# Pair 0 opens with its last 256 queries, and ScalarE's queue carries both one-hot rows

## The chip, the cores and the metric

The kernel runs on one core of one Trainium2 chip. The metric is device time in microseconds (us), the median of several executions of the whole kernel. Five engines work side by side, each on its own list of instructions in order: TensorE (PE in the profile, with PEld for its weight loads), VectorE (DVE), ScalarE (ACT), GpSimd (POOL) and SyncE (SP), which here only starts transfers. ACT and POOL start transfers too. An engine that has to wait for another's result holds up everything behind it in its own list. PSUM is the memory that TensorE writes its results to; it has eight banks of 512 fp32 values per partition.

## The reference, cut to what matters

Attention over 4 batches of 8 heads, 768 positions, head dimension 64, with a block mask, and then a mixer on its output:

```
scores = scale * q @ k.T                       # per batch and head, 768 x 768
mask   = |blk_i - blk_j| <= 1, or first/last block, or a sampled block   # blocks of 32
attn   = softmax(where(mask, scores, -1e9));   attn_out = attn @ v
u      = x + (U @ V applied over the sequence to x)      # x: heads side by side, rank 32
out    = u + relu(u @ w_ch1) @ w_ch2                     # 512 -> 2048 -> 512
```

Three random key blocks per query block (`sampled_blocks`) come in as data, so the mask is made on the chip.

## The kernel before, in words

**Pairs and units.** Two heads are handled together as a pair: 16 pairs, four of them (`HP`) to a batch. The diff touches pair 0, the first of all. The score matrix of a pair is computed transposed, keys on the partitions, in nine units (`NU`, `parts`, L474): with `tr, kind = divmod(u, 3)`, kinds 0 and 1 are one key tile of 128 against queries 0 to 511 (`QA`), and kind 2 is two key tiles against the last 256 queries (`QB`). A unit's scores for both heads fill one PSUM tile of 128 x 2 x 512 (`scores`, L480), two such tiles alternate during the first batch, and one exponential on ACT (L497) turns a unit into fp16 weights `est`. The values follow three units later (`VLAG`, `flush_value`, L898): 8 matmuls per unit against `vt`, accumulated in two PSUM buffers `pav`, one for queries 0 to 383 and one for 384 to 767. `norm` (L533) divides them by their row sums on DVE after the last two units.

**The mask.** In the first batch it is added inside the score matmul. The query operand `qa` has the head's 64 rows of q in one half of the partitions (`rows`) and in the other half (`mrows`) the mask rows, 24 per head: 0 where a query may look at a key block, -240 where it may not. The key operand `ka` has k in the one half and in the other the one-hot rows, which say which block a key belongs to. The one-hot rows are loaded from memory (`hot_rows`, L303); the mask rows come from a small matmul on PE (`mask_mm`, L374) of `cbd`, which DVE makes from `sampled_blocks`, into a PSUM tile `pm`, and are written to `qa` by DVE or ACT (`mask_rows`, L382). From the same two operands `mask_tiles` (L451) makes a mask `m01` of ones and zeros for the later batches: two matmuls `pmk` and two comparisons on DVE per key tile.

**How pair 0 starts.** q and k arrive as fp32 with positions on the partitions: `qld` in two loads, tiles 0 to 3 (`TQ`, 256 KB) and 4 to 5, `kld` in two loads, tiles 0 to 1 (`TK`) and 2 to 5. `cast0` (L326) makes fp16 copies `qst` and `kst` on DVE or POOL; PE turns them tile by tile into PSUM (`turn_some`, L263, into `pq` and `pk`); `half_copy` (L414) copies each head's half from there to `qa` or `ka`, on DVE or ACT. Unit 0 needs query tiles 0 to 3, key tile 0, the mask rows of queries 0 to 511 of both heads and both heads' one-hot rows. Matmuls named `warm` have no use but to keep PE busy.

**What sets the order.** Every engine's list is in program order (`keep`). In the first batch the loop at L1051 writes, for each pair and unit: the scores and the exponential, then the values of the unit three before, then the side work of `at_unit` (L983). In pair 0 that side work is: after unit 0 a warm matmul, the turns of the remaining q and k, the remaining mask rows, four half copies on DVE, then transfers on SP (`qa` mask rows to pair 1's `qa`, loads of pairs 2, U, V) and casts on POOL; after units 2, 3 and 8 a `mask_tiles`; after units 4 and 6 the turns of pair 1. The buffers of `pav`, and those of the turns, `pmk` and others (`ps`), rotate in the order of their requests (`pst_tile`, L109). From the second batch on a planner interleaves attention with the mixer's matmuls `pt` and `pch`; its lists are fixed when the program is built.

Of the kernel before, what the change touches and what calls it, by code (L numbers as in the profile page):

```python
# [17 lines left out]
P = 128  # L18
# [3 lines left out]
def kernel(  # L22
# [86 lines left out]
    def pst_tile(shape, dtype, name, tag):  # L109
        n = singles[tag][0]  # L110
        singles[tag].rotate(1)
        return psp[tag].tile(shape, dtype, tag=f"{tag}{n}", name=name)
# [150 lines left out]
    def turn_some(st, pt, t0, t1):  # L263
        for t in range(t0, t1):
            keep(
                nc.tensor.transpose(  # L266
                    out=pt[:, t, :],
                    in_=st[:, t].rearrange("p h d -> p (h d)"),
                    identity=id16,
                )  # L270
            )
# [31 lines left out]
    def hot_rows(eng, st, h, n):  # L303
        r0 = mrows[h].start
        keep(eng.dma_start(out=ka[st][h][r0 : r0 + n, :], in_=oh_dr.ap()[0:n]))
# [4 lines left out]
            in_=sampled_blocks.bitcast(I32),  # L310
        )
    )
    keep(nc.sync.dma_start(out=qld[:, :, 0:TQ], in_=q0[:, :, 0:TQ]))
    keep(nc.scalar.dma_start(out=small[0:32], in_=small_dr.ap()))
    keep(nc.scalar.dma_start(out=kld[:, :, 0:TK], in_=k0[:, :, 0:TK]))
    keep(nc.sync.dma_start(out=qld[:, :, TQ:T], in_=q0[:, :, TQ:T]))
    keep(nc.sync.dma_start(out=kld[:, :, TK:T], in_=k0[:, :, TK:T]))
    hot_rows(nc.scalar, 0, 0, NB)
    hot_rows(nc.sync, 0, 1, NB)
    keep(nc.scalar.activation(out=dummy, in_=zeros[:, 0:1], func=AF.Exp))  # L320
    for vt in vts:
        keep(nc.gpsimd.memset(vt[:, :, :, D : D + 1], 1.0))
# [3 lines left out]
    def cast0(eng, st, ld, t0, t1):  # L326
        keep(
            eng(
                out=st.rearrange("p t h d -> p h t d")[:, :, t0:t1],
                in_=ld[:, :, t0:t1],  # L330
            )
        )
# [41 lines left out]
    def mask_mm(o, a, e):  # L374
        mm(
            o,
            cbd.rearrange("z a c -> z (a c)"),
            small[:, a:e],
            True, True,
        )  # L380

    def mask_rows(eng, h, i, a, e):  # L382
        o = qa[0][h][mrows[h], a:e]
        if eng == "dve":
            keep(
                nc.vector.tensor_scalar(
                    out=o, in0=i[mrows[h]],
                    scalar1=-MASK_BIAS, scalar2=MASK_BIAS, op0=ALU.mult, op1=ALU.add,
                )
            )  # L390
        else:
            keep(
                nc.scalar.activation(
                    out=o, in_=i[mrows[h]],
                    func=AF.Copy, scale=-MASK_BIAS, bias=MASK_BIAS,
                )
            )

    pm0 = pscp.tile([P, 2, 512], FP32, tag="double0", name="pm")
    pm1 = pst_tile([P, QA], FP32, "pm", tag="pav")  # L400
    pm2 = pscp.tile([P, 2, 512], FP32, tag="double1", name="pm")
    mask_mm(pm0[:, 0, 0:QA], 0, QA)
    mask_mm(pm1, 0, QA)
    cast0(nc.vector.tensor_copy, qst, qld, 0, TQ)
    mask_rows("dve", 0, pm0[:, 0, 0:QA], 0, QA)
    mask_rows("act", 1, pm1, 0, QA)
    pq = pst_tile([P, T, P], FP16, "pturn", tag="ps")
    pk = pst_tile([P, T, P], FP16, "pturn", tag="ps")
    turn_some(qst, pq, 0, TQ)
    turn_some(kst, pk, 0, TK)  # L410
    mask_mm(pm2[:, 0, 0:QB], QA, S)
    warm_pe(2)

    def half_copy(eng, dst, h, pt, t0, t1):  # L414
        keep(
# [4 lines left out]
        )  # L420

    for h in range(2):
        half_copy(nc.vector.tensor_copy, qa[0], h, pq, 0, TQ)
        half_copy(nc.scalar.copy, ka[0], h, pk, 0, TK)
    cast0(nc.gpsimd.tensor_copy, qst, qld, TQ, T)
    cast0(nc.gpsimd.tensor_copy, kst, kld, TK, T)
    del lds[0, "q"], lds[0, "k"]
    for h in range(2):
# [38 lines left out]
    NU = 9  # L467
# [3 lines left out]
    def new_est():  # L471
        return epool.tile([P, 2, QA], FP16, tag="est", name="est")
# [93 lines left out]
    def new_pav(tag):  # L566
        return pst_tile([P, 3, 2, D + 1], FP32, "pav", tag)
# [330 lines left out]
    def flush_value():  # L898
        i, u, ests, pavs, xs, xh = pend.popleft()
        b, hp = divmod(i, HP)  # L900
        if u == 0:
            pavs.extend([new_pav("pav"), new_pav("pav")])
        for g, q0, q1, at in parts(u):
            for j in range(q0 // P, q1 // P):
                for h in range(2):
                    mm(
                        pavs[j // 3][:, j % 3, h, :],
                        weights(ests, g, j, h),
                        vts[b % 2][:, 2 * hp + h, g, 0 : D + 1],
                        u == 0 and j in (0, 3) and h == 0, g == T - 1, True,  # L910
                    )
        end = i == HP - 1
        if u == NU - 2:
            norm(i, 0, pavs[0], xs, xh, end)
        if u == NU - 1:
            norm(i, 1, pavs[1], xs, xh, end)
            box = {}
            uh = xpool.tile([P, T, P], FP16, tag="uh", name="uh")
            tails.extend(
                [  # L920
                    lambda: mix_a(i, xh, box, 0, "ps"),
                    lambda: mix_a(i, xh, box, 1, "ps"),
                    lambda: mix_h(i, 0, box["a"], xs, uh, "ps", end),
                    lambda: mix_h(i, 1, box["a"], xs, uh, "ps", end),
                ]
            )
            if end:
                tails.extend([lambda c=c: turn_u_half(i, uh, c) for c in range(2)])
            else:
                tails.append(lambda: turn_u_pe(i, uh, "ps"))  # L930
# [52 lines left out]
    def at_unit(i, u):  # L983
        if (i, u) in MASKS:
            mask_tiles(MASKS.index((i, u)))
        if i == 0:
            if u == 0:
                warm_pe(1)
                turn_some(qst, pq, TQ, T)
                turn_some(kst, pk, TK, T)  # L990
                for h in range(2):
                    mask_rows("dve", h, pm2[:, 0, 0:QB], QA, S)
                for nm, o, pt, t in (("q", qa[0], pq, TQ), ("k", ka[0], pk, TK)):
                    for h in range(2):
                        half_copy(nc.vector.tensor_copy, o, h, pt, t, T)
                for h in range(2):
                    keep(
                        nc.sync.dma_start(
                            out=qa[1][h][mrows[h], :], in_=qa[0][h][mrows[h], :]
                        )  # L1000
                    )
                issue(2, "q")
                keep(
                    nc.sync.dma_start(
                        out=uld, in_=moe_U.rearrange("(p t) r -> p (t r)", t=T)
                    )
                )
                issue(2, "k")
                for h in range(2):
                    keep(nc.sync.dma_start(out=mvld[h * R : h * R + R], in_=moe_V))  # L1010
                cast(1, "q")
                cast(1, "k")
                cast(1, "v")
            if u == 1:
                issue(2, "v")
            if u == 3:
                issue(3)
            if u == 6:
                cast(2, "q")
                cast_U()  # L1020
                cast(2, "k")
            if u == 4:
                turn_part(1, "q", 0)
                turn_part(1, "q", 1)
            if u == 6:
                turn_part(1, "k", 0)
                turn_part(1, "k", 1)
            return
        if u == 0 and i < 3:
            issue(i + 3)  # L1030
        if i == 1 and u == 2:
            cast_V()
            cast(2, "v")
        if i == 2 and u == 0:
            for h in range(2):
                keep(nc.sync.dma_start(out=Vd[rows[h]], in_=Vt[rows[0]]))
        if (i, u) in WLOADS:
            WLOADS[i, u]()
        if u in (1, 2, 3, 4):
            turn_part(i + 1, "qk"[(u - 1) // 2], (u - 1) % 2)  # L1040
        for _ in range({0: 1, 5: 2, 6: 1, 7: 1}.get(u, 0)):
            if tails:
                tails.popleft()()
        if u == 7:
            cast(i + 2, "q")
        if u == 8:
            cast(i + 2, "k")
        if u == 0 and i > 1:
            cast(i + 1, "v")

    for i in range(HP):  # L1051
        ests, pavs = [], []
        xs, xh = new_x()
        for u in range(NU):
            ests.append(new_est())
            scores(i, u, ests[u])
            pend.append((i, u, ests, pavs, xs, xh))
            if len(pend) > VLAG:
                flush_value()
            at_unit(i, u)  # L1060

# [197 lines left out]
```

## Time and profile before

| | us |
|---|---|
| median of 4 runs (lowest to highest) | 279.13 (278.54 to 279.55) |
| the profiled execution, and its span | 279.55, 277.8 |
| PE busy | 270.3 (97%) |
| DVE busy | 175.0 (63%) |
| ACT busy | 177.0 (64%) |
| POOL busy | 103.2 (37%) |
| first exponential of pair 0 starts | 8.31 |
| first `pt` matmuls (mixer, batch 0) | 45.62 |

The span is what the profile shows from its first to its last instruction; the profiled execution's time is 1.75 us more than it. In the lines that follow, a timeline row reads: start, duration, engine, line, operation, output<-inputs, shapes, and in brackets how long the engine was idle before and what ended that. `x2` means that two instructions are merged into the row. A row of the chain of waits reads: start, duration, what was waited for. A row of the stretches reads: from:to and length, then busy us (and instructions) of PE, PEld, DVE, ACT and POOL, the granted clock of PE, the busy share of the DMA engines and GB/s. "SPq" and "ACTq" mark a transfer's issue on that engine.

### The profile page before, as it was taken

The page shows a single profiled execution, that of the slowest core. Times are in us where ns is not written, and L with a number is a line of the kernel's source. Part 1 is how long each engine was busy: PE and PEld are TensorE (multiplying, and loading weights), DVE is VectorE, ACT ScalarE, POOL GpSimd, SP SyncE. Part 2 cuts the span into 40 slices and gives each one's busy share as a digit, 9 for nine tenths or more (in the row PEclk, how much of TensorE's full clock was granted, in tenths as well). Part 3 has the DMA queues.
Part 4 walks back from the last instruction along what each step waited for, and adds up shares of the span by engine and source line. Part 5 has one row for each costly group of instructions (what it writes and reads, how often), then busy time and mean ns, then how long its engine had stood idle before and what let it go on. Part 6 is the DMA issues. An engine that isn't in the chain of part 4 may idle for free.

```text
span 277.8 us, 8036 instructions
## 1 busy us (share of the span) xinstructions
PE 270.3 (97%) x3492; PEld 161.5 (58%) x3492; DVE 175.0 (63%) x285; ACT 177.0 (64%) x198; POOL 103.2 (37%) x137
## 2 busy tenths in 40 slices
PE   7899999999999999999999999999999999999995
PEld 2577775566656564657565565656565655565443
DVE  6767767888887987777756768777777441000112
ACT  4799996787987857694855749584886201654000
POOL 4669539406374735363604536361102020000000
PEclk9999999999999999999999999999999999999999
DMA  6999966999979999996890999995100323000222
GB/s 185 297 284 287 282 145 92 186 179 75 142 49 96 181 130 139 160 103 74 64 108 0 184 92 167 132 97 75 31 2 2 104 79 93 13 1 0 78 76 77
DMA packets 85520, 31.69 MB, mean 114 GB/s; under 512 B 75164, under 2 KB 83084, under 8 KB 85484
## 3 DMA queue, kind: packets, MB, share of 16 engines
q0 software_dynamic: 49824, 10.29, 43.2%
q1 hardware_dynamic: 35304, 20.66, 34.6%
q8 instruction: 27, 0.44, 0.7%
q10 hardware_dynamic: 356, 0.22, 0.3%
q14 instruction: 9, 0.07, 0.1%
HBM read 27.88 MB, written 6.29 MB: 123 GB/s over the span
## 4 chain that ended last, share of the span: by engine, by line
PE 92%; ACT 2%; DMA 2%; DVE 2%; POOL 1%; issue 1%; DVEq 0%; POOLq 0%
PE pch L173 30%; PE pt L173 30%; PE psc L173 14%; PE pav L173 13%; ACT est L497 2%; PE pa L173 2%; DMA ka<-onehot_const 2%; PE ph L173 1%; PE pturn L266 1%; PE pmk L173 1%; POOL xh L597 0%; PE puT L710 0%; DVE xh L540 0%; DVE xs L588 0%; POOL qst L247 0%
## 5 line engine op out<-in xcount | busy, mean ns | idle before, releaser
L497 ACT ACTIVATE est<-psc 128x1024 f16<-128x1024 f32 x144 | 143.0, 1028 | 46.3 <-PE psc L173 44.7
L173 PE MATMUL pt<-uT,w1t 64*128 64x384 f16 (+1 forms) x896 | 94.4, 324 | 0.0
L173 PE MATMUL pch<-w2t,tT 64*128 64x512 f16 (+3 forms) x688 | 93.6, 372 | 0.1
L518 DVE TENSOR_TENSOR est<-est,m 128x1024 f16<-128x1024 f16 x108 | 78.3, 740 | 18.1 <-ACT est L497 16.8
L173 PEld LDWEIGHTS <-w1t 64*128 64x128 f16 (+1 forms) x896 | 46.0, 95 | 36.2 <-PE pt L173 8.3
L173 PEld LDWEIGHTS <-tT 64*128 64x128 f16 (+1 forms) x688 | 38.2, 95 | 36.9 <-PE pch L173 1.6
L735 ACT ACTIVATE tT<-pt 128x768 f16<-128x768 f32 (+1 forms) x48 | 36.6, 773 | 26.0 <-PE pt L173 26.0
L173 PEld LDWEIGHTS <-est 128*128 128x128 f16 x1152 | 41.4, 97 | 10.9 <-issue 5.0
L173 PE MATMUL pav<-vt,est 128*128 128x65 f16 x1152 | 44.5, 193 | 0.1
L790 DVE TENSOR_TENSOR of<-xf,pch 128x1024 f32<-128x1024 f32 (+3 forms) x16 | 15.2, 951 | 42.7 <-PE pch L173 42.7
L173 PE MATMUL psc<-qT,kT 64*128 64x512 f16 (+1 forms) x288 | 40.6, 323 | 0.3 <-ACT est L497 0.3
L597 POOL CAST xh<-xs 128x768 f16<-128x768 f32 x12 | 10.4, 869 | 80.2 <-DVE xs L588 74.6
L683 POOL CAST uh<-xf 128x768 f16<-128x768 f32 x12 | 13.9, 1161 | 26.1 <-DVE xf L674 14.5
L173 PE MATMUL psc<-qa,ka 128*128 128x512 f16 (+1 forms) x96 | 21.7, 326 | 1.7 <-DMA ka<-onehot_const 1.3
L737 DVE TENSOR_SCALAR tT<-pt 128x768 f16<-128x768 f32 (+1 forms) x20 | 18.3, 917 | 5.9 <-PE pt L173 5.8
L173 PEld LDWEIGHTS <-kT 64*128 64x128 f16 x288 | 14.6, 94 | 12.5 <-issue 0.7
L261 POOL DMA_DIRECT2D vt<-in_v_dram x20 | 16.3, 820 | 2.8 <-DMA w2t<-in_moe_w_ch_dram 2.7
L261 POOL DMA_DIRECT2D qst<-in_q_dram x20 | 16.3, 819 | 0.1
L261 POOL DMA_DIRECT2D kst<-in_k_dram x20 | 16.3, 820 | 0.0
L588 DVE TENSOR_TENSOR xs<-pav,rcp 128x768 f32<-128x768 f32 x12 | 11.5, 958 | 1.2
L674 DVE TENSOR_TENSOR xf<-xs,ph 128x768 f32<-128x768 f32 x12 | 11.4, 951 | 1.2 <-PE ph L173 1.2
L173 PEld LDWEIGHTS <-ka 128*128 128x128 f16 (+1 forms) x108 | 8.7, 97 | 5.3 <-issue 3.7
(69 smaller groups left out, 129.6 us busy)
## 6 DMA issues: line engine op xcount, KB each, us to landing
out_dram<-of SPq DMA_DIRECT2D x9, 512.0 KB, 3.3
vld<-in_v_dram SPq DMA_DIRECT2D x6, 384.0 KB, 7.5
w1t<-in_moe_w_ch_dram POOLq DMA_DIRECT2D x4, 512.0 KB, 8.6
w2t<-in_moe_w_ch_dram POOLq DMA_DIRECT2D x4, 512.0 KB, 10.1
qld<-in_q_dram SPq DMA_DIRECT2D x5, 384.0 KB, 7.0
kld<-in_k_dram SPq DMA_DIRECT2D x5, 384.0 KB, 7.9
qst<-in_q_dram POOLq DMA_DIRECT2D x20, 96.0 KB, 4.1
kst<-in_k_dram POOLq DMA_DIRECT2D x20, 96.0 KB, 4.4
```

Source lines behind the costliest of these rows:

```text
L173: ins = nc.tensor.matmul(out, lhsT, rhs, start=start, stop=stop, skip_group_check=loose)
L261: keep(nc.gpsimd.dma_start(out=o[:, h], in_=src_of(nm, i)[:, h]))
L266: nc.tensor.transpose(out=pt[:, t, :], in_=st[:, t].rearrange("p h d -> p (h d)"), identity=id16,)
L497: keep(nc.scalar.activation(out=est, in_=psc, func=AF.Exp, scale=0.125))
L518: keep(nc.vector.tensor_tensor(out=o, in0=o, in1=m, op=ALU.mult))
L588: nc.vector.tensor_tensor(out=xs.rearrange("p (c j) (h d) -> p c (j h) d", c=2, h=2), in0=pv[:, :, :, 0:D], in1=rcp[:, :, :, None].broadca ...
L597: keep(nc.gpsimd.tensor_copy(out=xh, in_=xs))
L674: nc.vector.tensor_tensor(out=u.rearrange("p (c j) n -> p c j n", c=2), in0=xs.rearrange("p (c j) n -> p c j n", c=2), in1=ph[:, :, 0:HS]. ...
L683: keep(nc.gpsimd.tensor_copy(out=uh, in_=u))
L735: keep(nc.scalar.activation(out=o, in_=i, func=AF.Relu))
L737: keep(nc.vector.tensor_scalar_max(out=o, in0=i, scalar1=0.0))
L790: nc.vector.tensor_add(out=of, in0=xfs[b][:, sc : sc + nsc, n0:n1], in1=pch)
```

## The change

Pair 0's units run in the order 2, 0, 1, 3, 4, ... 8; the side work stays with the position in that order. So the first scores are those of key tiles 0 and 1 against queries 512 to 767, and the parts of q change places: tiles 4 and 5 are loaded first, cast by DVE and turned before the first scores; tiles 0 to 3 are cast by POOL and turned after them. The turns and copies of k's last four tiles move from the first position to the second. The one-hot rows of both heads are loaded from ACT's queue. ACT writes the mask rows of queries 0 to 511 for both heads, from one PSUM tile, so one mask matmul of 512 columns goes; DVE writes those of queries 512 to 767 for both, now before the first scores. One warm matmul moves. `pavs` becomes a dictionary whose buffers are requested when first written.

```diff
-    keep(nc.sync.dma_start(out=qld[:, :, 0:TQ], in_=q0[:, :, 0:TQ]))
+    keep(nc.sync.dma_start(out=qld[:, :, TQ:T], in_=q0[:, :, TQ:T]))
     keep(nc.scalar.dma_start(out=small[0:32], in_=small_dr.ap()))
     keep(nc.scalar.dma_start(out=kld[:, :, 0:TK], in_=k0[:, :, 0:TK]))
-    keep(nc.sync.dma_start(out=qld[:, :, TQ:T], in_=q0[:, :, TQ:T]))
+    keep(nc.sync.dma_start(out=qld[:, :, 0:TQ], in_=q0[:, :, 0:TQ]))
     keep(nc.sync.dma_start(out=kld[:, :, TK:T], in_=k0[:, :, TK:T]))
-    hot_rows(nc.scalar, 0, 0, NB)
-    hot_rows(nc.sync, 0, 1, NB)
+    for h in range(2):
+        hot_rows(nc.scalar, 0, h, NB)
...
-    pm0 = pscp.tile([P, 2, 512], FP32, tag="double0", name="pm")
-    pm1 = pst_tile([P, QA], FP32, "pm", tag="pav")
-    pm2 = pscp.tile([P, 2, 512], FP32, tag="double1", name="pm")
+    pm2 = pst_tile([P, QB], FP32, "pm", tag="pav")
+    pm0 = pscp.tile([P, 2, 512], FP32, tag="double1", name="pm")
+    mask_mm(pm2, QA, S)
     mask_mm(pm0[:, 0, 0:QA], 0, QA)
-    mask_mm(pm1, 0, QA)
-    cast0(nc.vector.tensor_copy, qst, qld, 0, TQ)
-    mask_rows("dve", 0, pm0[:, 0, 0:QA], 0, QA)
-    mask_rows("act", 1, pm1, 0, QA)
+    mask_rows("dve", 0, pm2, QA, S)
+    for h in range(2):
+        mask_rows("act", h, pm0[:, 0, 0:QA], 0, QA)
+    cast0(nc.vector.tensor_copy, qst, qld, TQ, T)
+    mask_rows("dve", 1, pm2, QA, S)
...
-    turn_some(qst, pq, 0, TQ)
+    warm_pe(1)
+    turn_some(qst, pq, TQ, T)
     turn_some(kst, pk, 0, TK)
-    mask_mm(pm2[:, 0, 0:QB], QA, S)
-    warm_pe(2)
+    warm_pe(1)
...
-        half_copy(nc.vector.tensor_copy, qa[0], h, pq, 0, TQ)
+        half_copy(nc.vector.tensor_copy, qa[0], h, pq, TQ, T)
         half_copy(nc.scalar.copy, ka[0], h, pk, 0, TK)
-    cast0(nc.gpsimd.tensor_copy, qst, qld, TQ, T)
+    cast0(nc.gpsimd.tensor_copy, qst, qld, 0, TQ)
...
-        if u == 0:
-            pavs.extend([new_pav("pav"), new_pav("pav")])
...
+                    opens = j // 3 not in pavs
+                    if opens:
+                        pavs[j // 3] = new_pav("pav")
...
-                        u == 0 and j in (0, 3) and h == 0, g == T - 1, True,
+                        opens, g == T - 1, True,
...
             if u == 0:
                 warm_pe(1)
-                turn_some(qst, pq, TQ, T)
-                turn_some(kst, pk, TK, T)
+                turn_some(qst, pq, 0, TQ)
                 for h in range(2):
-                    mask_rows("dve", h, pm2[:, 0, 0:QB], QA, S)
-                for nm, o, pt, t in (("q", qa[0], pq, TQ), ("k", ka[0], pk, TK)):
-                    for h in range(2):
-                        half_copy(nc.vector.tensor_copy, o, h, pt, t, T)
+                    half_copy(nc.vector.tensor_copy, qa[0], h, pq, 0, TQ)
...
             if u == 1:
+                turn_some(kst, pk, TK, T)
+                for h in range(2):
+                    half_copy(nc.vector.tensor_copy, ka[0], h, pk, TK, T)
                 issue(2, "v")
...
-        ests, pavs = [], []
+        ests, pavs = {}, {}
         xs, xh = new_x()
-        for u in range(NU):
-            ests.append(new_est())
+        for n, u in enumerate((2, 0, 1, *range(3, NU)) if i == 0 else range(NU)):
+            ests[u] = new_est()
             scores(i, u, ests[u])
...
-            at_unit(i, u)
+            at_unit(i, n)
```

## The prediction

> **What bounds the kernel now.** I read part 1 of the page (PE 270.3 of 277.8 us), then the stretches, then the chain of waits from the start in order of time, then the timelines of ACT, PE and DVE up to 12 us, where the diff lies. One row of the stretches:
>
> ```profile
> 48.40:277.80 229.40, 225.66 (x2927) 131.97 (x2926) 140.97 (x207) 136.79 (x153) 70.96 (x83) 1.00 0.77 91
> ```
>
> After 48.4 us PE is busy 225.66 of 229.40 us at full clock, with the same instructions in both kernels. So whatever the change does to the moment when PE gets there moves the end by as much. Before it, 36 exponentials on ACT go in step with PE: two PSUM tiles alternate, so unit n+2's scores wait for exp n. The chain from the start:
>
> ```profile
> 2.77 4.99 DMA ka<-onehot_const
> 7.76 0.14 issue
> 7.90 0.39 PE psc L173
> 8.29 0.02 issue
> 8.31 1.03 ACT est L497
> 9.35 0.04 issue
> 9.39 0.60 PE psc L173 x4
> ```
>
> The first exp starts at 8.31 because head 1's one-hot rows, issued by SP at 2.77, land 4.99 us later. ACT up to there:
>
> ```profile
> 1.88 0.59 ACTq L305 DMA_DIRECT2D ka<-onehot_const  x1
> 2.50 1.28 ACT L320 ACT_TABLE_LOAD   x1 [2.50 <-DVE ka L287]
> 3.79 0.20 ACT L320 ACTIVATE dummy<-m 128x1 f16<-128x1 f16 x1
> 4.85 0.59 ACT L393 ACTIVATE qa<-pm 64x512 f16<-64x512 f32 x1 [0.86 <-PE pm L173]
> 5.71 0.76 ACT L416 COPY ka<-pturn 64x256 f16<-64x256 f16 x2 [0.27 <-PE pturn L266]
> 8.31 4.97 ACT L497 ACTIVATE est<-psc 128x1024 f16<-128x1024 f32 x5 [1.84 <-PE psc L173]
> ```
>
> ACT's operands were ready at 6.47 (5.71 + 0.76) and it idled 1.84 us. Next PE, then DVE, behind that first exp:
>
> ```profile
> 8.11 0.38 PE L173 MATMUL warm<-m 128*128 128x512 f16 x1
> 8.33 0.27 PE L266 MATMUL pturn<-id,qst 128*128 128x128 f16 x2
> 8.44 0.39 PE L266 MATMUL pturn<-id,kst 128*128 128x128 f16 x4
> ```
>
> ```profile
> 8.64 0.61 DVE L416 COPY qa<-pturn 64x256 f16<-64x256 f16 x2 [1.18 <-PE pturn L266]
> 9.28 0.86 DVE L416 COPY ka<-pturn 64x512 f16<-64x512 f16 x2
> 10.29 1.02 DVE L459 TENSOR_SCALAR m<-pmk 128x384 f16<-128x384 f32 x2 [0.15 <-PE pmk L173]
> ```
>
> The reader should see here that the exps after the first are fed by DVE. The two key copies (9.28, 0.86) end at 10.14; the second pmk matmul and the scores of key tile 2 (10.46) stand behind them on PE, and the fourth exp follows at 11.11 (10.46, 0.61 for its two score matmuls, 0.04 to ACT), 0.97 after the copies. I call that end of the copies D.
>
> **The change, part by part.** First the moment K at which ACT ends the second ka copy.
>
> Second one-hot on ACT's queue: one more issue of 0.59. In the build it waits on the semaphore of the first load (small, landed 0.73 + 1.9 = 2.63 by the DMA view), so it runs 2.66 to 3.25. Behind it on ACT stand the table load (1.28, to 4.56) and dummy (0.20, to 4.77). The old cover, 0.86 us of ACT idle before L393, is gone.
>
> Mask rows 0..511 of both heads on ACT: two of 0.59 with 0.03 between starts and ends, to 6.01. Then the two ka copies, 0.76: K = 6.77. The spacing of dependent-free ACT work has two rows: the copies do not overlap (two in 0.76, each 0.36), exps do (1.02 long, next 0.92 later). Three overlaps of 0.1 would give 6.47, which is also the floor set by the key turns (5.71 + 0.76). I take 6.77, from the copies: same engine, same half of the partitions, PSUM source. ScalarE: Activation LUTs, section What ACT_TABLE_LOAD costs, says that back-to-back ACTIVATEs overlap by about 93 ns; the exps agree and the copies do not. By that rule K would be 6.49, and the sum below about 0.23 instead of 0.51.
>
> The landing of that one-hot: the first one on ACT's queue, issued at 1.88, was there when its reader started its weights at 6.13, so at most 4.25 us; by it the second lands by 6.91, by SP's row (4.99) at 7.65. PE needs it at K + 0.03. A landing at 6.91 would add 0.11 (start 0.14 after it, as 7.90 after 7.76); I take 0, since 6.13 was set by ACT's copy and not by the landing; 7.65 is kept for a rival. DMA: Bandwidth & Descriptors, section Issuing engines are not separate DMA queues, says that transfers of all issuing engines share the same 16 DMA engines and another issuer saves only issue time. That speaks against this move: by it the row keeps SP's 4.99, and the sum would be that of the rival, 1.36.
>
> SP loses one issue (0.43) and swaps its two q loads: the last 128 KB go first, the 256 KB land by 1.73 + 3.7 = 5.43. Its qa-to-qa copies wait for mask rows ready at 6.01 instead of 7.0. All SP work behind moves earlier; it feeds pair 1, whose first scores are at 16.3. I cost this at nothing.
>
> POOL casts the 512-element q part (0.61, the row of the same form) instead of 0.40: 5.43 to 6.05, needed by PE at K + 0.72 = 7.49. Its rest of k lands at 2.26 + 5.1 = 7.36, cast to 8.0, needed at 9.2. Two one-hot issues (1.21) and v (0.83) end at 10.1, first value matmul about 11.2. So over 1 us of cover each; a load over 1 us late would come through in full.
>
> DVE's early work: two masks 64x256 (0.42), a cast (at most 0.43), two copies (0.29 each), 1.9 us from about 4.4, done by 6.3, beside ACT. PE's removed 512-column mask matmul and moved warm matmuls lie before K, in time that PE idles. They do keep it busy: PE's first six warm matmuls take 0.46 each (2.74 in all), those from 5.62 on start 0.22 apart. Before, PE had six warm and two mask matmuls by 4.82; now it has six, 256 and 512 columns and one more warm in about the same time, so I use the fast rows. If PE were still slow, the 2,816 columns from K to D would take twice their 1.2 us.
>
> Now from K to D, each from a row:
> K + 0.17 head 1's first score (6.09 to 6.26 before); three 256-column starts of 0.11 (four take 0.60, one 0.27): 0.50; warm 0.22 (8.11 to 8.33): 0.72; four q turns 0.39 and 0.04 to DVE: 1.15; two 64x512 q copies 0.87: 2.02; head 1's scores of unit 0 0.17: 2.19 (second exp 0.41 later, K + 2.60 = 9.37); matmul spacing 0.22: 2.41; four k turns 0.39 and 0.04: 2.84; two k copies 0.86: 3.70. D = 6.77 + 3.70 = 10.47, against 10.14: **0.33 later**. The first exp starts early, at 7.46 (K + 0.50, 0.16 left of the last matmul's 0.27, 0.03 to ACT), but what is late next is unit 0: its turns now stand behind the first scores, its copies behind them, and the k turns behind its scores. Ends: K at 6.47 gives 0.03, a one-hot at 6.91 gives 0.44.
>
> Masks, values and later units keep their order, and PE runs without a gap from the fourth unit's scores at 10.46 to 12.23, so the 0.33 is carried.
>
> The value accumulators: pair 0 now opens the half of queries 384.. first, so it gets the first buffer, normalised last. Before, pair 1's first values:
>
> ```profile
> 19.52 0.18 PE pav L173 x6
> 19.70 0.04 issue
> 19.74 0.24 PE pav L173 x2
> ```
>
> Six matmuls ran while DVE finished, two waited. Now the six use the late buffer and all eight wait: **0.18 more**. Ends: 0 if DVE is done early; 0.76 if the reciprocal (0.20) and multiply (0.56) both stand open. I take 0.18, since DVE's order is unchanged. PE has no gap after it to give it back: the chain of waits runs on PE, piece on piece, from 15.3 to 39.9.
>
> Sum: 0.33 + 0.18 = **0.51 us**. The profiled execution would go from 279.55 (span 277.8 and 1.75 around it) to 280.06; it stood 0.42 above the median of 279.13, so the median goes to 279.64. About 0.3% (0.84 us) is what a measurement of this kernel can tell from no change; 0.51 is 0.18%.
>
> **Rivals.** *The one-hot lands late* (slower). At 7.65, head 1's first score starts 0.14 after it, 7.79 instead of 6.94: 0.85 more, in all 1.36, 280.5. For it: SP's row, 4.99. Against: SP's rows stood behind 640 KB of q and k, ACT's behind 179 KB. It decides from a landing after 6.8.
>
> *Pair 1 waits for the whole normalisation* (slower). 0.76 in place of 0.18: 1.09 in all, 280.2. For it: PE and ACT have no slack there. Against: the values come after unit 3's scores, which already hide most of it.
>
> *PE still slow at K* (slower): 1.2 more, in all 1.7, 280.8; for and against as above.
>
> *The first exp's lead is kept* (faster). At K = 6.47 it starts at 7.16, 1.15 before 8.31; less 0.18, 0.97 gained, 278.2. For it: ACT idled 1.84 us for this one row. Against: the second exp must follow within 0.92 for that, and the count above puts it 1.9 later.
>
> **How the numbers follow.** Forecast 0.52, late one-hot 0.20, whole normalisation 0.10, slow PE 0.05, lead kept 0.13. The forecast's own range is 279.1 to 280.1 (K from 6.47 to 6.9, spread of the medians); some 0.08 of its chance lies over 279.97. So within 0.3%: 0.44; slower 0.08 + 0.20 + 0.10 + 0.05 = 0.43; faster 0.13. The range of 8 in 10 goes from 278.5, which leaves out most of the faster case, to 280.8, past the late one-hot with 0.3 for spread and up to the slow PE.
>
> **What the profile after would show.** First exp near 7.5 and ACT idle about 0.9 before the second, near 9.4; k copies on DVE ending near 10.5; fourth exp near 11.45 (before 11.11); eight pav together after DVE in pair 1; the tail from the first pt matmuls 0.5 later. A first exp beyond 8 would show the late one-hot; k copies ending before 10.1 would show the lead kept. I would be wrong as well if a load behind POOL's casts came more than 1 us later.

## The result, and the profile after

| | before | changed |
|---|---|---|
| median (lowest to highest), us | 279.14 (278.36 to 280.62), 79 runs | 279.71 (279.28 to 282.53), 53 runs |
| profiled execution, and its span | 279.55, 277.8 | 279.76, 278.0 |
| PE busy, us | 270.3 | 270.2 |
| first exponential starts | 8.31 | 7.41 |
| 36th exponential, the last of pair 3, starts | 41.69 | 41.90 |

The ratio is 1.003, with a 95% interval of 1.0021 to 1.0039: slower by 0.57 us by the medians, where 0.51 was forecast (279.64). The means lie 0.83 us apart (280.04 and 279.21), which is the 0.3% of the ratio, because some executions of the changed kernel run late at a lower granted clock; they are treated with the warm matmuls below.

The row of the stretches of the changed kernel from 48.6 us on, PE's columns alone (busy us and instructions, granted clock, busy share of the DMA engines, GB/s):

```profile
48.60:278.00 229.40, 225.68 (x2927) 1.00 0.78 91
```

It answers to the row 48.40 to 277.80 of before: as many instructions and as much busy time in as long a stretch, 0.2 later. All of the difference is made before it. It also holds across the kernels below that ran at full clock: each profiled execution's time is its 36th exponential's start plus 237.86 to 237.93 us (41.69 and 279.55 before, 41.90 and 279.76 after, 40.69 and 278.55 for the fastest). So what follows is read from the starts of 36 exponentials.

ACT's timeline of the changed kernel:

```profile
1.86 1.00 ACTq L305 DMA_DIRECT2D ka<-onehot_const  x2
2.89 1.28 ACT L320 ACT_TABLE_LOAD   x1 [2.89 <-DMA w1t<-small_const]
...
4.63 1.21 ACT L393 ACTIVATE qa<-pm 64x512 f16<-64x512 f32 x2 [0.24 <-PE pm L173]
5.74 0.74 ACT L418 COPY ka<-pturn 64x256 f16<-64x256 f16 x2
7.41 1.02 ACT L499 ACTIVATE est<-psc 128x1024 f16<-128x1024 f32 x1 [0.92 <-PE psc L173]
9.19 1.94 ACT L499 ACTIVATE est<-psc 128x1024 f16<-128x1024 f32 x2 [0.76 <-PE psc L173]
11.30 2.07 ACT L499 ACTIVATE est<-psc 128x1024 f16<-128x1024 f32 x2 [0.18 <-PE psc L173]
```

The idle times in brackets are what to read: before, ACT idled 1.84 us ahead of the first exponential and then ran on without a gap (five in the row shown). Now it idles 0.92, 0.76 and 0.18. The first exponential came 0.90 earlier, and the fourth (11.30) 0.18 later. The chain of waits says why:

```profile
2.56 4.18 DMA ka<-onehot_const
6.75 0.14 issue
6.88 0.49 PE psc L173 x3
7.37 0.21 PE warm L173
7.58 0.24 PE pturn L266 x4
...
7.85 0.42 DVE qa L418
...
8.29 0.44 DVE qa L418
...
8.77 0.38 PE psc L173
9.15 0.24 PE pturn L266 x4
...
9.48 0.42 DVE ka L418
...
9.91 0.44 DVE ka L418
```

Head 1's one-hot row lands at 6.75 and gates the first scores. Behind them stand unit 0's four turns of q and their two copies, unit 0's scores, four turns of k and their two copies, in one line up to 10.35. The exponentials wait at each handover from DVE.

Later, in pair 1's fifth unit, the chain reads:

```profile
18.74 0.26 PE pav L173 x8
...
19.02 0.21 DVE rcp L537
...
19.25 0.57 DVE xs L542
...
19.86 0.42 PE pav L173 x8
```

All eight value matmuls stand behind the normalisation's multiply (`xs`), where before six ran while it finished and two waited.

### The profile page after: what moved, and what is told of

Same layout as the page of the kernel before. It is cut to its first block, busy times and chain, and to the rows that moved or that the text cites. A ratio compares the mean times of both kernels' runs of the same rounds, so it can differ in the third digit from the quotient of the medians.

```text
span 278.0 us, 8034 instructions
## 1 busy us (share of the span) xinstructions
PE 270.2 (97%) x3491; PEld 161.4 (58%) x3491; DVE 174.2 (63%) x284; ACT 177.7 (64%) x199; POOL 103.4 (37%) x137
## 4 chain that ended last, share of the span: by engine, by line
PE 85%; ACT 8%; DVE 2%; DMA 2%; issue 1%; POOL 0%; DVEq 0%; POOLq 0%
PE pch L173 30%; PE pt L173 30%; PE pav L173 11%; PE psc L173 10%; ACT est L499 8%; PE pa L173 2%; DMA ka<-onehot_const 2%; PE ph L173 1%; DMA w1t<-small_const 1%; POOL xh L599 0%; PE pmk L173 0%; DVE xh L542 0%; DVE xs L590 0%; DVE ka L418 0%; DVE qa L418 0%
## 5 line engine op out<-in xcount | busy, mean ns | idle before, releaser
L173 PE MATMUL psc<-qa,ka 128*128 128x256 f16 (+1 forms) x96 | 21.8, 326 | 1.7 <-ACT ka L418 0.5
```

The source lines that it names most:

```text
L173: ins = nc.tensor.matmul(out, lhsT, rhs, start=start, stop=stop, skip_group_check=loose)
```

## The experiments

The table has, for each profiled execution, the start of the first exponential, some distances between starts, and the distance from the first to the 36th. The smallest values in a column (0.98, 0.90, 0.90, 0.94) are taken as those with no added wait. "Time" is that execution's own.

| kernel | first | to 2nd | 3rd to 4th | 11th to 12th | 13th to 14th | 1st to 36th | 36th | time |
|---|---|---|---|---|---|---|---|---|
| before | 8.31 | 0.98 | 0.90 | 0.90 | 0.94 | 33.38 | 41.69 | 279.55 |
| before, second trace | 7.55 | 0.98 | 0.90 | 1.03 | 1.06 | 33.63 | 41.18 | 279.06 |
| both rows on ACT | 7.27 | 1.28 | 0.90 | 1.60 | 1.04 | 34.11 | 41.38 | 279.25 |
| changed | 7.41 | 1.78 | 1.20 | 0.90 | 1.12 | 34.49 | 41.90 | 279.76 |
| one row back on SP | 7.10 | 1.78 | 1.20 | 0.90 | 1.22 | 34.38 | 41.48 | 279.34 |
| buffers as before | 7.73 | 1.78 | 1.20 | 0.90 | 0.94 | 34.30 | 42.03 | 279.90 |
| k turned earlier | 7.47 | 1.78 | 0.90 | 0.90 | 1.12 | 34.07 | 41.54 | 279.43 |
| both undone, PE warmer | 7.53 | 1.78 | 0.90 | 0.90 | 0.94 | 33.88 | 41.41 | 279.29 |
| both rows on ACT, loads swapped | 7.15 | 1.64 | 0.90 | 0.90 | 0.94 | 33.54 | 40.69 | 278.55 |

**The kernel before once more** (no edit), to see whether its one profiled execution was typical.

> The kernel before, a second time, to see how far one trace of it stands for its runs. Theory A (the handover alone): the time is within 0.1% of before; its first exp starts within 0.3 us of 8.31 and the key copies on DVE end within 0.3 of 10.14, so the change's trace (10.35) is 0.2 later for good. Rival B (the profiled execution of before was a slow one): the one-hot rows on SP's queue land earlier here, the first exp starts before 8.0 and the key copies end before 9.9, so that the change costs 0.5 or more at that point. Rival C (PE's clock): the executions' granted clock stays above 0.995 in nearly all of them, where about a fifth of the changed kernel's lay between 0.988 and 0.994.

Measured: 279.33 (278.45 to 280.33, 12 runs), ratio 1.001 [0.9993, 1.0027]; the profiled execution took 279.06. DVE's copies in its timeline (in the first trace they began at 8.64 and 9.28):

```profile
7.88 0.61 DVE L416 COPY qa<-pturn 64x256 f16<-64x256 f16 x2 [0.61 <-PE pturn L266]
8.52 0.86 DVE L416 COPY ka<-pturn 64x512 f16<-64x512 f16 x2
```

Head 1's row, again from SP, landed 4.20 us after its issue (7.01) instead of 4.99 (7.76), and the whole front came 0.76 earlier: the key copies end at 9.38, not 10.14. At the 36th exponential only 0.51 of it is left. Its chain shows where the rest went:

```profile
8.13 8.16 DMA qld<-in_q_dram
...
16.43 0.84 POOL qst L247
...
17.32 0.34 PE pturn L266 x3
```

The load of pair 2's q, issued at 8.13, takes 8.16 us; POOL casts it, and PE's turns, in its list ahead of pair 1's third scores, wait. That holds the 12th exponential 0.12 back, and 0.11 more goes at the 14th, where the chain runs over DVE's normalisation. So before had been profiled in one of its later starts. By the constant above, its median of 279.14 stands for a 36th exponential near 41.27, close to this trace.

**Both one-hot rows on ACT's queue, and nothing else**, on the kernel before:

```diff
-    hot_rows(nc.scalar, 0, 0, NB)
-    hot_rows(nc.sync, 0, 1, NB)
+    for h in range(2):
+        hot_rows(nc.scalar, 0, h, NB)
```

> Of the change only both one-hot rows on ACT's queue; units 0, 1, 2 as before. Theory A: the row lands near 6.75 as in the changed kernel, the first exp starts near 7.3 instead of 8.31; the turns of k now wait for POOL's cast of k (8.0), the key copies end near 9.4 instead of 10.14, and the kernel is 0.3 to 0.5 us faster than before. Rival (the queue move is itself the loss): ACT's extra issue delays its mask row, the first exp stays at 8.2 or later, and the time is that of before or up to 0.5 us more.

Measured: 279.0 (278.04 to 279.54), ratio 0.9988 [0.9971, 1.0005]. The row landed at 6.38 and the first exponential began at 7.27, but the second came 1.28 behind it (the rest of k landed at 6.97, and POOL cast it until 7.64), and then in pair 1, on PE's and POOL's timelines:

```profile
17.84 0.34 PE L266 MATMUL pturn<-id,qst 128*128 128x128 f16 x3 [0.83 <-POOL qst L247]
```

```profile
16.96 0.83 POOL L247 CAST qst<-qld 128x768 f16<-128x768 f32 x1 [2.94 <-PE pav L173]
```

PE stood still for 0.83 us for pair 2's q. POOL's brackets name a `pav` matmul as what ended the idle time, but the cast takes nothing from it, and such releasers are inferred. What the cast takes is the load of pair 2's q: by the trace's semaphore counts it landed at 16.81, 0.15 before the cast, as in the second trace of before (16.29, and the cast at 16.43). The last experiment, which brings that load forward, agrees. Against the second trace of before the early row is worth 0.28 at the first exponential, and that is gone at the second (8.55 against 8.53); the load then costs more than it did there. In the times no gain and no loss can be told.

**The changed kernel with the buffers in the old order**:

```diff
     def flush_value():
...
+        if not pavs:
+            for c in range(2):
+                pavs[c] = new_pav("pav")
...
-                    opens = j // 3 not in pavs
-                    if opens:
-                        pavs[j // 3] = new_pav("pav")
+                    opens = (j // 3, "open") not in pavs
+                    pavs[j // 3, "open"] = True
```

> The changed kernel with the two value buffers requested in the old order (queries 0 to 383 first). Theory A: pair 1's first values run as six and then two again, its fifth exp comes 0.18 us earlier relative to pair 0, and the time falls 0.18 us against the changed kernel. Rival: the wait moves to the second buffer, and nothing changes.

Measured: 279.52 (279.15 to 281.5), ratio 1.003 [1.001, 1.005]. The 13th and 14th exponentials are 0.94 apart instead of 1.12, and from the 13th to the 36th it is 21.91 against 22.11. So in the trace the buffer's wait costs 0.18, and it is not given back by the 36th exponential. The median is 0.19 lower, but twelve executions don't tell that from chance: the ratio to before is 1.003, as that of the changed kernel. The profiled execution itself was late for another reason: its row landed at 7.07.

**The changed kernel with k's last turns and copies at the first position**, as before the change:

```diff
             if u == 0:
...
                 for h in range(2):
                     half_copy(nc.vector.tensor_copy, qa[0], h, pq, 0, TQ)
+                turn_some(kst, pk, TK, T)
+                for h in range(2):
+                    half_copy(nc.vector.tensor_copy, ka[0], h, pk, TK, T)
...
             if u == 1:
-                turn_some(kst, pk, TK, T)
-                for h in range(2):
-                    half_copy(nc.vector.tensor_copy, ka[0], h, pk, TK, T)
```

> The changed kernel with the turns and copies of k's last four tiles put back to the first position, behind the q turns and ahead of unit 0's scores. Theory A (the handover: k's turns behind unit 0's scores make DVE's key copies late): the key copies end at 9.6 to 10.0 instead of 10.35 to 10.67, the fourth exp follows the third without a wait (0.92 instead of 1.20 between them), and the time is 0.3 us under the changed kernel, 0.1% over before. Rival (the exps after the second are held by something else, PE's own work or the loads): the copies end earlier, but the 36th exp and the time stay within 0.1 us.

Measured: 279.42 (278.96 to 280.34), ratio 1.0023 [1.0007, 1.0038]. DVE's timeline:

```profile
7.91 0.88 DVE L418 COPY qa<-pturn 64x512 f16<-64x512 f16 x2 [1.86 <-PE pturn L266]
8.82 0.86 DVE L418 COPY ka<-pturn 64x512 f16<-64x512 f16 x2
```

The key copies follow the query copies at once and end at 9.68, not 10.34; the fourth exponential comes 0.90 behind the third, not 1.20. The fifth comes another 0.12 sooner behind the fourth (0.93 instead of 1.05), so the distance from the first to the 36th falls by 0.42. The median is 0.29 lower; the intervals of the two ratios overlap, so by the times alone this isn't shown. The second exponential still comes 1.78 after the first: that gap belongs to the order of the units.

**The changed kernel with head 1's row back on SP's queue**:

```diff
-    for h in range(2):
-        hot_rows(nc.scalar, 0, h, NB)
+    hot_rows(nc.scalar, 0, 0, NB)
+    hot_rows(nc.sync, 0, 1, NB)
```

> The changed kernel with head 1's one-hot row back on SP's queue, as before. Theory A: the two traces of the kernel before had that row down 4.2 and 5.0 us after its issue on SP, those with both rows on ACT 3.8 to 4.5 after theirs, so the queue hardly matters: it lands between 6.8 and 7.8 (7.0 likeliest), ACT's mask rows come 0.3 earlier, the first exp starts within 0.3 of 7.6, the time is the changed kernel's within 0.15. Rival (the ACT queue is what makes the row early): it lands 0.8 or more later, and so do the first exp and the end.

Measured: 279.57 (279.34 to 281.54), ratio 1.0027 [1.001, 1.0044]. The chain of waits:

```profile
2.79 3.33 DMA ka<-onehot_const
6.12 0.05 issue
6.17 0.89 PE psc L173 x4
```

From SP, behind the same loads, the row lands 3.33 us after its issue, sooner than any from ACT's queue that the chain times (4.18, 4.24, 4.33, 4.39 and 4.48 in kernels with the new order). SP's three are 4.99, 4.20 and 3.33, on both sides of ACT's. So no advantage of either queue can be told; one trace's landing is one draw from a spread of over 1.5 us.

**The changed kernel with four warm matmuls more** (two behind the first turns, ahead of the first scores, and two behind unit 0's turns), run twice:

```diff
     turn_some(kst, pk, 0, TK)
-    warm_pe(1)
+    warm_pe(3)
...
                 turn_some(qst, pq, 0, TQ)
+                warm_pe(2)
```

> The changed kernel with two more warm matmuls before the first scores and two after the turns of the last q tiles, both in time that PE idles. Theory A (the handover alone): the trace is the same within 0.1 us and so is the median. Rival C (PE's clock falls back in some executions, because PE is busy only 0.4 to 0.8 of each us from 5 to 9): the executions over 280.4 and with a granted clock under 0.995, about a quarter of the changed kernel's, become rare, the mean falls by 0.3 us or more, the median by 0.1 to 0.2.

> The changed kernel with the four more warm matmuls, a second time. Rival C (PE's clock falls back when PE does too little in a stretch of the first 10 us): again none of some twelve executions below a granted clock of 0.995 and none over 280.5. Theory A (the handover alone) gives the share of the changed kernel, 12 of 66, so two or so here.

**The same with two warm matmuls fewer** than the changed kernel:

```diff
     turn_some(kst, pk, 0, TK)
-    warm_pe(1)
...
             if u == 0:
-                warm_pe(1)
                 turn_some(qst, pq, 0, TQ)
```

> The changed kernel without two of its warm matmuls: that after the first k turns and that at the first position. Rival C (PE's clock): half or more of the executions show a granted clock of 0.988 to 0.995 and lie 1.3 to 1.6 us above the rest, so the median rises by 0.5 to 1.5 us. Theory A (the handover alone): k's turns and the copies behind the first scores come 0.2 us earlier for want of the warm matmul ahead of them, and the time falls by 0.1 to 0.2 us.

These three are about something that the profiled execution of the changed kernel doesn't show. In 9 of its 54 executions with a clock on record PE's mean granted clock was 0.988 to 0.994, and their median is 281.11; the other 45 have 279.62. With four warm matmuls more the medians are 279.71 and 279.70, ratios 1.0023 [1.0008, 1.0038] and 1.002 [1.0004, 1.0035], and none of 24 executions has a lower clock (highest time 280.33). With two fewer it is 6 of 9, and the median 280.38, ratio 1.0049 [1.0027, 1.0071]. Its profiled execution, at 281.79, is one of the six. The stretches (PE's busy us and instructions, granted clock, DMA share, GB/s):

```profile
5.00:6.00 1.00, 0.40 (x4) 1.00 0.77 222
6.00:7.00 1.00, 0.37 (x2) 1.00 1.03 340
7.00:8.00 1.00, 0.63 (x7) 0.91 1.07 296
8.00:9.00 1.00, 0.87 (x3) 0.50 1.01 376
...
13.00:14.00 1.00, 1.00 (x7) 0.50 1.08 256
14.00:15.00 1.00, 1.00 (x16) 0.68 1.08 271
15.00:16.00 1.00, 1.00 (x19) 1.00 1.10 240
```

and its chain, whose steps answer to those of the changed kernel:

```profile
8.13 1.04 PE psc L173 x2
9.18 0.43 PE pturn L266 x4
9.60 0.85 PE psc L173 x2
10.46 0.67 PE pmk L173 x2
```

After two stretches in which PE was busy 40% and 37%, the clock is half for 6.8 us (a mean of 0.91 in 7 to 8 means half clock from 7.82 on, and 0.68 in 14 to 15 means until 14.64). PE takes 1.04 for two score matmuls, and the path runs over PE alone; the 36th exponential starts at 43.89. Half clock for 6.8 of 280 us makes a mean of 0.988, for half as long 0.994: the two ends of what the nine executions had. The changed kernel's own trace, at full clock, comes close to these shares of busy time; its PE columns:

```profile
5.00:6.00 1.00, 0.61 (x5) 1.00 0.91 276
6.00:7.00 1.00, 0.40 (x3) 1.00 1.02 329
7.00:8.00 1.00, 0.81 (x8) 1.00 1.06 343
```

The other kernels had 3 of 12 (buffers as before), 0 of 12 (k turned earlier, with which PE has four turns more at this place), 0 of 12 (one row back on SP) and, of the kernel before beside these runs, 1 of 106. Without added warm matmuls the new order thus has 12 of 90, with them 0 of 36, the combined kernel below included. So warm matmuls take these executions away, but not the 0.5 us by which the median is later: another effect.

**Buffers as before, k turned earlier and four warm matmuls more, all in the changed kernel**:

> The changed kernel with three things undone or added: k's last turns back at the first position, the value buffers in the old order, four more warm matmuls. Theory A (the terms are independent): 0.29 (measured for the k turns) and 0.18 (the buffers) come off the changed kernel, which gives 279.15 to 279.25, 0.1% over before, and no execution has a granted clock under 0.995. Rival (they overlap): 279.4, as with the k turns alone.

Measured: 279.23 (278.86 to 279.65), ratio 1.0006 [0.9993, 1.0019]. The two waits are gone in the trace (0.90 and 0.94 in the table), and the loss with them: the interval lies below that of the changed kernel. What is left of the change, the other unit first and the rows on ACT, is worth nothing that can be told.

**Pair 2's q ahead of pair 1's v**, on the kernel with both rows on ACT's queue:

```diff
-    issue(1)
+    issue(1, "qk")
...
                 issue(2, "q")
+                issue(1, "v")
...
                 cast(1, "k")
-                cast(1, "v")
...
                 cast(2, "q")
+                cast(1, "v")
```

> The kernel before with both one-hot rows on ACT's queue, and pair 1's v loaded behind pair 2's q and cast behind it, instead of ahead. Theory D (in the kernel before an early first exp is given back at pair 1's third unit, which waits for pair 2's q: load of 8.16 us, cast, turns): POOL's cast of pair 2's q starts near 15 instead of 16.4 to 17.0, pair 1's third exp follows its second after 0.90 to 0.92 instead of 1.03 to 1.60, and the kernel is 0.3 to 0.7 us faster than before. Rival: the load is as late, since the queues are full, or the later v or the mask rows' copies hold pair 1 up elsewhere, and the time is within 0.2 of before.

> The kernel before with both one-hot rows on ScalarE's queue and pair 1's v loaded and cast behind pair 2's q, once more, for a tighter interval. The first look had a median of 278.64 with a ratio of 0.9983 [0.9964, 1.0001]. If the swap of the loads is worth what its trace showed (the 36th exponential at 40.69 against 41.18 in the second trace of before, some 0.5 us), the median is 278.5 to 278.8 and the interval of the ratio stays under 1. The rival, that the first look was a lucky draw of landing times: 278.9 to 279.2, with the interval around 1.

Measured: 278.64 (278.13 to 279.86), ratio 0.9983 [0.9964, 1.0001], and the second time 278.87 (278.27 to 282.1), ratio 0.9997 [0.9975, 1.0019]. POOL's timeline in the first:

```profile
14.10 0.83 POOL L247 CAST qst<-qld 128x768 f16<-128x768 f32 x1 [1.40 <-DMA qld<-in_q_dram]
15.82 0.83 POOL L241 CAST vt<-vld 128x768 f16<-128x768 f32 x1 [0.89 <-DMA vld<-in_v_dram]
```

The cast of pair 2's q starts at 14.10 (16.96 without the swap, 16.43 in the second trace of before), and pair 1 has no wait left in either trace: 0.90 and 0.94. The medians are 0.38 and 0.43 under those of before that ran with them, the lowest of all kernels here, but both intervals reach 1. A likely gain of about 0.4 us, not a shown one; one of the 24 executions had the lower clock (282.1). Not all of the lead in the traces (40.69 against 41.18 at the 36th) is pair 2's load: both traces of before also have 1.24 from the 33rd to the 34th exponential, where these two have 0.93. A wait near there is absent in four of the 13 traces, and its cause stays open.

## Why the prediction was right, and where it was not

The size and the sign held, and the two terms behind them show in the traces when they are taken out one at a time: 0.29 at the fourth exponential (0.42 up to the 36th) for k's turns and copies, 0.18 for the buffer. In the times only the kernel without both, and with warm matmuls added, is clear of noise: it is back at the time of before.

**K and the row, two errors that cancelled.** K was put at 6.77. ACT ended its copies at 6.48 (5.74 + 0.74): the second row's issue took about 0.30, not 0.59 (two in 1.00), of which a wait of 0.24 for PE's `pm` took a part back, and the copies began 0.10 before the mask rows ended. The Trainium skill, page ScalarE: Activation LUTs, section What ACT_TABLE_LOAD costs, says that such instructions overlap by about 93 ns; the second mask row and the first copy agree here, the two mask rows (1.21 for two of 0.59) and the two copies (0.74 for two) among themselves do not, and I had taken all of them without overlap. But the row, whose landing I let cost 0, came at 6.75 and set head 1's score at 6.88, against 6.94 foretold. First exponential 7.41 (7.46), second 9.19 (9.37), key copies ended 10.34 (10.47), fourth 11.30 (11.45).

**The count from the first scores to D.** From head 1's score it is 3.46 by the trace, 3.53 by my count. This is the part that carried the forecast: the beginnings and ends of DVE's copies lie within 0.07 of the count, and only the second exponential came 0.12 sooner.

**The buffer.** 0.18 was foretold and measured, at the place named.

**The base of the sum failed.** The step was: the profiled execution "stood 0.42 above the median", so the median moves by the same 0.51. That took the 0.42 for something that the change leaves alone. It was the landing of head 1's row at 7.76, which is the very thing that the change touches. Against that trace the changed kernel lost 0.18 at the fourth exponential and 0.21 at the 36th, less than foretold; against the second trace of before it lost 0.94 and 0.72. By the table it is: 0.80 lost between the first and second exponential (1.78 less 0.98), 0.29 before the fourth, 0.18 in pair 1, 1.27 in all, of which 0.16 comes back in small pieces, at the fifth exponential and near the 34th (34.49 less 33.38 is 1.11); the first exponential is 0.90 earlier than in the one trace of before and 0.14 than in the other. In the second, 0.25 of its lead goes in pair 1, where PE waits for pair 2's load. So 0.51 was a small loss reckoned on a late start with a give-back left out; the measured 0.57 is a large loss on an earlier start, with some given back. The agreement to 0.06 is better than the reasoning was.

**The load behind POOL's casts.** I wrote that a late load would show, and looked for it in the changed kernel, where none came. It shows in before: where the first exponential is early, pair 2's q is what ends the wait in pair 1. I had read "PE has no gap" from one late start, in which that load was hidden.

**The rivals.** The row's landing does set the first exponential, as the late one-hot had it, but it came at 6.12 to 7.07 in the changed kernels whose chain times it, not at 7.65: I had priced that rival with the latest draw. The Trainium skill, DMA: Bandwidth & Descriptors, section Issuing engines are not separate DMA queues, spoke against a gain from the other queue; the 3.33 us from SP's agrees with it, the 4.99 was not SP's price. The whole normalisation did not come through (0.18, not 0.76). PE did slow down in a sixth of the executions, and in the one trace that has it (two warm matmuls fewer) behind the first scores instead of at K: I had given it 0.05, as if it held for all or none. The lead was not kept, for the reason given: the second exponential would have had to follow within 0.92, and came 1.78 behind.

## What to carry to other kernels

Before a sum is made against one profiled execution, ask whether what makes it stand off the median is the wait that the change touches; if it is, that distance must not be carried over, and a second trace of the same kernel is worth more than another term. In a start where the engines hand work to one another, an earlier first result is worth nothing if the second stands behind a longer line: count to the first unit from which the engines run without a gap. Where units are reordered, look at what else is requested in that order: here a buffer rotation cost 0.18 us in the next pair, far from the edit.

## What the runs showed of the hardware

Head 1's one-hot row, 36 KB at the start of the kernel, landed 3.33 to 4.99 us after its issue from SP's queue (three traces) and 3.82 to 4.48 us from ACT's (ten traces, by the semaphore counts); in the kernel before, with no edit, this moved the first exponential by 0.76 us.

With two warm matmuls fewer PE's granted clock fell to half for 6.8 us, behind stretches of 1 us with PE busy 40, 37 and 63%, though from its first matmul on PE's longest idle time before it was 0.71 us. The Trainium skill, TensorE: Matmul & The Clock Gate, section HAM oscillation — how this bites in real kernels, warns of idle gaps over some 3.4 us; here no such gap was there: in this trace a stretch of short gaps was enough. It cost 1.1 to 1.5 us, by the medians of the executions with and without it (280.42 against 279.29 with two warm matmuls fewer, 281.11 against 279.62 as changed). The number of warm matmuls moves the share of executions in which it happens: 6 of 9, 9 of 54, and 0 of 24 for two fewer, as changed, and four more.

The issues of both one-hot rows on ACT, one behind the other, took 1.00 us, where a single one took 0.59.
